# Packing a 64-wide remainder tile into two column halves of TensorE, with a new head and tail, in a two-GEMM SiLU kernel

## Chip, cores and metric

One core of a Trainium2 chip. The metric is the device time of one execution in microseconds (us). An execution with a profile also gives a span, from its first to its last instruction; here the time is about 1.8 us longer than the span (134.19 against 132.4 before).

## The reference

```python
B, S, D, F = 1, 2048, 640, 1728        # all bf16
def reference(x, w1, w2):
    h = jnp.einsum("bsd,df->bsf", x, w1)
    h = silu(h)
    return jnp.einsum("bsf,fd->bsd", h, w2)
```

F = 1728 is 13 tiles of 128 and one of 64. This remainder is what the change is about.

## The kernel before

A scheduler orders the instructions of each engine and sets the waits. The parts that matter (cuts marked):

```python
WARM_MMS = 10
...
zt = wpool.tile([P, 512], dt_in, name="zt")
nc.vector.memset(zt[:], 0.0)
for i in range(WARM_MMS):                      # keep TensorE busy until x has landed
    nc.tensor.matmul(ps_w[:, :], lhsT=zt[:, 0:P], rhs=zt[:, :], ...)
nc.vector.memset(w1_sb[:, :, F:F_PAD], 0.0)    # the 14th tile is padded from 64 to 128
nc.gpsimd.memset(w2_sb[F_REM:P, FT - 1, :], 0.0)
# head: x rows 0-511, then w1 in pieces of 384 columns, then the other x by transposing DMA
for dt in range(DT):                           # DT = 5
    ... four 128x128 transposes into psT (two buffers) ...
    if k % 2 == 0: nc.vector.tensor_copy(out=dst, in_=psT[:, :])
    else:          nc.scalar.activation(out=dst, in_=psT[:, :], func=ACT.Copy)
# first GEMM: 4 chunks of 512 rows x FT = 14 tiles x 5 matmuls
for (s0, w) in g1_chunks:
    for ft in range(FT):
        for dt in range(DT):
            nc.tensor.matmul(ps[:, :w], lhsT=w1_sb[:, dt, f0 : f0 + P],
                             rhs=xT_sb[:, dt, s0 : s0 + w], ...)
        nc.scalar.activation(out=sig[:, :w], in_=ps[:, :w], func=ACT.Sigmoid)
        nc.vector.tensor_tensor(out=gT_sb[:, ft, s0 : s0 + w], in0=ps[:, :w], in1=sig[:, :w], op=ALU.mult)
# second GEMM: 16 row blocks x 2 halves of 320 columns x 14 matmuls
for st in range(ST):
    for ci, (e0, en) in enumerate(e_chunks):
        for ft in range(FT):
            nc.tensor.matmul(ps2[:, :en], lhsT=gT_sb[:, ft, s0 : s0 + P],
                             rhs=w2_sb[:, ft, e0 : e0 + en], ...)
        ... evict on ScalarE (ci 0) or VectorE (ci 1) ...
    nc.sync.dma_start(out=of[s0 : s0 + P, :], in_=o_sb[:])
```

## Time and profile before

| | before |
|---|---|
| time, median | 134.19 us (6 runs when I predicted; 133.94 us over 16 runs later) |
| span of the profiled execution | 132.4 us |
| busy: PE, DVE, ACT | 127.7, 48.4, 43.2 us |
| PE idle before its two large groups | 0.0 us |

PE is TensorE, PEld its weight loads, DVE VectorE, ACT ScalarE, POOL GpSimd, SP SyncE; a "q" behind a name is the engine's sequencer, and "issue" is time in which the engine waited for nothing that the profile shows. A busy PE says little by itself, since matmuls overlap one another (one of 512 columns is recorded as 379 ns long, and the next starts 216 ns after it). The useful lines are the chain that ended last and the spacing of the matmuls in it. The prediction quotes and reads them.

TensorE begins at a slower pace. The ten warm-ups of 512 columns took 424 ns each, against 216 later, and transposes start 107 ns apart up to 6.21 us and 55 ns apart from 6.61 on. In between, at 6.36 us, the trace's raw record of the granted clock at full speed begins. This is the "rise of the clock" below; "cold" is before it. What sets its time is not shown.

### The profile page before, as it was taken

The page shows a single profiled execution, that of the slowest core. Times are in us where ns is not written, and L with a number is a line of the kernel's source. Part 1 is how long each engine was busy: PE and PEld are TensorE (multiplying, and loading weights), DVE is VectorE, ACT ScalarE, POOL GpSimd, SP SyncE. Part 2 cuts the span into 40 slices and gives each one's busy share as a digit, 9 for nine tenths or more (in the row PEclk, how much of TensorE's full clock was granted, in tenths as well). Part 3 has the DMA queues.
Part 4 walks back from the last instruction along what each step waited for, and adds up shares of the span by engine and source line. Part 5 has one row for each costly group of instructions (what it writes and reads, how often), then busy time and mean ns, then how long its engine had stood idle before and what let it go on. Part 6 is the DMA issues. An engine that isn't in the chain of part 4 may idle for free.

```text
span 132.4 us, 1881 instructions
## 1 busy us (share of the span) xinstructions
PE 127.7 (96%) x758; PEld 74.2 (56%) x758; DVE 48.4 (37%) x78; ACT 43.2 (33%) x76; POOL 1.3 (1%) x7
## 2 busy tenths in 40 slices
PE   6999999999999999999999999999999999999990
PEld 2454444444444444444457777777777777777760
DVE  1136666666666666666661001111110111111101
ACT  4055555555555555555551111100111111011110
POOL 4000000000000000000000000000000000000000
PEclk9999999999999999999999999999999999999999
DMA  3999446549900000000000111110011111101111
GB/s 89 353 330 228 104 104 60 117 92 290 357 9 2 0 5 2 0 0 0 0 0 5 50 50 50 50 51 18 35 50 50 50 54 50 49 2 48 54 50 50
DMA packets 16040, 9.78 MB, mean 74 GB/s; under 512 B 9184, under 2 KB 16032, under 8 KB 16032
## 3 DMA queue, kind: packets, MB, share of 16 engines
q1 hardware_dynamic: 16032, 9.67, 25.8%
q8 instruction: 6, 0.10, 0.3%
q14 instruction: 2, 0.02, 0.0%
HBM read 5.08 MB, written 2.62 MB: 58 GB/s over the span
## 4 chain that ended last, share of the span: by engine, by line
PE 96%; DVE 1%; issue 0%; DVEq 0%
PE ps L193 46%; PE ps L171 46%; PE ps L90 3%; PE psT L147 1%; DVE o_sb L203 0%; DVE xT_sb L154 0%; DVE zt L87 0%; DVE warm L77 0%; DVEq L203 0%
## 5 line engine op out<-in xcount | busy, mean ns | idle before, releaser
L193 PE MATMUL ps<-w_sb,gT_sb 128*128 128x320 bf16 x448 | 61.0, 299 | 0.0
L171 PE MATMUL ps<-xT_sb,w_sb 128*128 128x512 bf16 x280 | 60.9, 379 | 0.0
L193 PEld LDWEIGHTS <-gT_sb 128*128 128x128 bf16 x448 | 43.8, 98 | 17.2
L180 DVE TENSOR_TENSOR gT_sb<-ps,sig 128x512 bf16<-128x512 f32 x56 | 38.8, 692 | 22.5 <-ACT sig L179 22.5
L171 PEld LDWEIGHTS <-w_sb 128*128 128x128 bf16 x280 | 27.3, 98 | 32.8 <-issue 0.2
L179 ACT ACTIVATE sig<-ps 128x512 bf16<-128x512 f32 x56 | 33.5, 598 | 27.2 <-PE ps L171 27.2
L203 DVE CAST o_sb<-ps 128x320 bf16<-128x320 f32 x16 | 7.9, 492 | 52.2 <-PE ps L193 52.2
L201 ACT ACTIVATE o_sb<-ps 128x320 bf16<-128x320 f32 x16 | 7.0, 438 | 51.8 <-PE ps L193 51.8
L90 PE MATMUL ps<-zt 128*128 128x512 bf16 x10 | 4.4, 631 | 1.2 <-DVE zt L87 1.2
L154 DVE COPY xT_sb<-psT 128x512 bf16<-128x512 bf16 x3 | 1.3, 425 | 5.7 <-PE psT L147 5.7
L90 PEld LDWEIGHTS <-zt 128*128 128x128 bf16 x10 | 1.3, 143 | 3.4 <-issue 2.2
L156 ACT ACTIVATE xT_sb<-psT 128x512 bf16<-128x512 bf16 x2 | 1.2, 598 | 4.8 <-PE psT L147 4.8
L147 PEld LDWEIGHTS <-xn_sb 128*128 128x128 bf16 x20 | 1.8, 118 | 1.2 <-issue 0.8
L147 PE MATMUL psT<-ident,xn_sb 128*128 128x128 bf16 x20 | 2.1, 255 | 0.1
L78 ACT ACT_TABLE_LOAD x1 | 1.3, 1283 | 0.7 <-PEq L219 0.7
L101 POOL MEMSET w_sb<- 64x640 bf16 x1 | 0.6, 632 | 0.1
L77 DVE MEMSET warm<- 128x4 f32 x1 | 0.1, 62 | 0.8 <-PEq L219 0.8
masks.py:199 POOL TENSOR_SCALAR_AFFINE_SELECT ident<-ident 128x128 bf16<-128x128 bf16 x1 | 0.3, 294 | 0.1
L87 DVE MEMSET zt<- 128x256 uint32 x1 | 0.3, 272 | 0.0
L78 ACT ACTIVATE warm<-warm 128x4 f32<-128x4 f32 x1 | 0.2, 206 | 0.0
masks.py:197 POOL MEMSET ident<- 128x128 bf16 x1 | 0.2, 205 | 0.3 <-POOLq L219 0.3
L99 DVE MEMSET w_sb<- 128x160 uint32 x1 | 0.2, 192 | 0.0
(4 smaller groups left out, 0.4 us busy)
## 6 DMA issues: line engine op xcount, KB each, us to landing
out_dram<-o_sb SPq DMA_DIRECT2D x16, 160.0 KB, 1.8
w_sb<-in_w_dram SPq DMA_DIRECT2D x1, 2080.0 KB, 9.0
w_sb<-in_w_dram SPq DMA_DIRECT2D x4, 480.0 KB, 6.7
xn_sb<-in_x_dram SPq DMA_DIRECT2D x1, 640.0 KB, 4.3
w_sb<-in_w_dram SPq DMA_DIRECT2D x1, 240.0 KB, 7.0
xT_sb<-in_x_dram SPq DMA_TRANSPOSE x15, 2.8
w_sb<-in_w_dram SPq DMA_DIRECT2D x1, 80.0 KB, 8.6
```

Source lines behind the costliest of these rows:

```text
L78: nc.scalar.activation(out=warm[:], in_=warm[:], func=ACT.Sigmoid)
L90: nc.tensor.matmul(ps_w[:, :], lhsT=zt[:, 0:P], rhs=zt[:, :], start=(i == 0), stop=(i == WARM_MMS - 1),)
L101: nc.gpsimd.memset(w2_sb[F_REM:P, FT - 1, :], 0.0)
L147: nc.tensor.transpose(out=psT[:, i * P : (i + 1) * P], in_=xn_sb[:, sa // P + i, dt * P : (dt + 1) * P], identity=ident[:, :],)
L154: nc.vector.tensor_copy(out=dst, in_=psT[:, :])
L156: nc.scalar.activation(out=dst, in_=psT[:, :], func=ACT.Copy)
L171: nc.tensor.matmul(ps[:, :w], lhsT=w1_sb[:, dt, f0 : f0 + P], rhs=xT_sb[:, dt, s0 : s0 + w], start=(dt == 0), stop=(dt == DT - 1),)
L179: nc.scalar.activation(out=sig[:, :w], in_=ps[:, :w], func=ACT.Sigmoid)
L180: nc.vector.tensor_tensor(out=gT_sb[:, ft, s0 : s0 + w], in0=ps[:, :w], in1=sig[:, :w], op=ALU.mult,)
L193: nc.tensor.matmul(ps2[:, :en], lhsT=gT_sb[:, ft, s0 : s0 + P], rhs=w2_sb[:, ft, e0 : e0 + en], start=(ft == 0), stop=(ft == FT - 1),)
L201: nc.scalar.activation(out=o_sb[:, e0 : e0 + en], in_=ps2[:, :en], func=ACT.Copy)
L203: nc.vector.tensor_copy(out=o_sb[:, e0 : e0 + en], in_=ps2[:, :en])
```

## The change

It intends to (1) compute the 64-wide tile of two chunks at the same time, in the two column halves of the array; (2) shorten the head, with fewer warm-up matmuls, a smaller first piece of w1 and all copies of transposed x on VectorE; (3) shorten the tail by splitting the last row block into 512 and 128 columns with a store each. The second GEMM gets a second copy of w2's remainder, `w2b_sb`, zero in partitions 0 to 63, for the chunks whose remainder now lies in partitions 64 to 127. The core of the diff (many cuts, marked):

```diff
-WARM_MMS = 10
-W1_PIECE_COLS = 384
+WARM_MMS = 8
+W1_PIECES = [128, 256, 384, 384]
+LAST_ST_SPLIT = [512, 128]
...
-        nc.vector.memset(zt[:], 0.0)
+        nc.gpsimd.iota(zt32[:], pattern=[[1, max(P, WARM_N) // 2]], base=1, channel_multiplier=P)
...
+        if PST_COPY_ACT and k % 2 == 1:          # PST_COPY_ACT = 0
+            nc.scalar.activation(out=dst, in_=psT[:, :], func=ACT.Copy)
+        else:
+            nc.vector.tensor_copy(out=dst, in_=psT[:, :])
...
+    for (ca, cb) in pairs:                        # (1, 2) and (3, 0)
+        ps_p = psum1.tile([P, 512], mybir.dt.float32, name="ps1")
+        for dt in range(DT):
+            for h, s0 in ((0, sa), (HP, sb)):     # HP = 64
+                nc.tensor.matmul(
+                    ps_p[h : h + HP, :],
+                    lhsT=w1_sb[:, dt, fl * P : fl * P + HP],
+                    rhs=xT_sb[:, dt, s0 : s0 + 512], ...)
+        ... one sigmoid and one multiply for both halves, into gP ...
...
+                if ft < fl:
+                    lh = gT_sb[:, ft, s0 : s0 + P]
+                    rh = w2_sb[:, ft, e0 : e0 + en]
+                else:
+                    g, k = where[s0 // 512]
+                    lh = g[:, s0 % 512 : s0 % 512 + P]
+                    rh = (w2b_sb if k else w2_sb[:, fl, :])[:, e0 : e0 + en]
...
+            if st == last_st:
+                nc.sync.dma_start(out=of[s0 : s0 + P, e0 : e0 + en], in_=o_sb[:, e0 : e0 + en])
```

More of the change, by code (lines that the diff above doesn't have):

```diff
@@ L10 @@
 ALU = mybir.AluOpType
-WARM_MMS = 10
-C0_SUB = 512
-W1_PIECE_COLS = 384
-PE_TRANSPOSE_CHUNK0 = 1
+WARM_MMS = 8
+WARM_N = 512
+W1_PIECES = [128, 256, 384, 384]
+LAST_ST_SPLIT = [512, 128]
+COLPACK = 1
+PST_COPY_ACT = 0
 @with_exitstack
@@ L28 @@
     P = nc.NUM_PARTITIONS
+    HP = P // 2
     xf = x.flatten_outer_dims()
@@ L42 @@
     dt_in = x.dtype
+    dup = F_REM == HP
     chunks = []
@@ L52 @@
     c0_tiles = wc0 // P
-    c0_sub = min(wc0, max(P, (C0_SUB // P) * P)) if PE_TRANSPOSE_CHUNK0 else wc0
-    assert wc0 % c0_sub == 0
+    pairs = []
+    if COLPACK and dup and len(chunks) % 2 == 0 and all(w == 512 for _, w in chunks):
+        order = list(range(1, len(chunks))) + [0]
+        for i in range(0, len(order), 2):
+            pairs.append((order[i], order[i + 1]))
+    packed_chunks = set(c for pr in pairs for c in pr)
     e_chunks = []
@@ L62 @@
         e += n
+    if LAST_ST_SPLIT and sum(LAST_ST_SPLIT) == D and all(v % 32 == 0 and 0 < v <= 512 for v in LAST_ST_SPLIT):
+        e_chunks_last = []
+        e = 0
+        for v in LAST_ST_SPLIT:
+            e_chunks_last.append((e, v))
+            e += v
+    else:
+        e_chunks_last = e_chunks
     wpool = ctx.enter_context(tc.tile_pool(name="wpool", bufs=1))
@@ L74 @@
     gT_sb = gpool.tile([P, FT, S], dt_in, name="gT_sb")
+    ident = wpool.tile([P, P], dt_in, name="ident")
+    make_identity(nc, ident)
+    xn_sb = wpool.tile([P, c0_tiles, D], dt_in, name="xn_sb")
+    if WARM_MMS > 0:
+        zt32 = wpool.tile([P, max(P, WARM_N) // 2], mybir.dt.int32, name="zt32")
+        nc.gpsimd.iota(zt32[:], pattern=[[1, max(P, WARM_N) // 2]], base=1, channel_multiplier=P)
+        zt = zt32.bitcast(dt_in)
+        ps_w = psum2.tile([P, 512], mybir.dt.float32, name="ps2")
+        for i in range(WARM_MMS):
+            nc.tensor.matmul(
+                ps_w[:, :WARM_N],
+                lhsT=zt[:, 0:P],
+                rhs=zt[:, :WARM_N],
+                start=(i == 0),
+                stop=(i == WARM_MMS - 1),
+            )
     warm = wpool.tile([P, 4], mybir.dt.float32, name="warm")
@@ L78 @@
     nc.scalar.activation(out=warm[:], in_=warm[:], func=ACT.Sigmoid)
-    if PE_TRANSPOSE_CHUNK0:
-        ident = wpool.tile([P, P], dt_in, name="ident")
-        make_identity(nc, ident)
-        xn_sb = wpool.tile([P, c0_tiles, D], dt_in, name="xn_sb")
-    if WARM_MMS > 0:
-        zt = wpool.tile([P, 512], dt_in, name="zt")
-        nc.vector.memset(zt[:], 0.0)
-        ps_w = psum2.tile([P, 512], mybir.dt.float32, name="ps2")
-        for i in range(WARM_MMS):
-            nc.tensor.matmul(
-                ps_w[:, :],
-                lhsT=zt[:, 0:P],
-                rhs=zt[:, :],
-                start=(i == 0),
-                stop=(i == WARM_MMS - 1),
-            )
-    if F_PAD > F:
+    if F_PAD > F and not dup:
         nc.vector.memset(w1_sb[:, :, F:F_PAD], 0.0)
@@ L101 @@
         nc.gpsimd.memset(w2_sb[F_REM:P, FT - 1, :], 0.0)
+    w2b_sb = wpool.tile([P, D], dt_in, name="w2b_sb")
+    nc.gpsimd.memset(w2b_sb[0:HP, :], 0.0)
     x3 = xf.rearrange("s (dt p) -> s dt p", p=P)
-    if PE_TRANSPOSE_CHUNK0:
-        for sa in range(0, wc0, c0_sub):
-            sb = sa + c0_sub
-            nc.sync.dma_start(
-                out=xn_sb[:, sa // P : sb // P, :],
-                in_=xf[s0c0 + sa : s0c0 + sb, :].rearrange("(st p) d -> p st d", p=P),
-            )
-    else:
-        for dt in range(DT):
-            nc.sync.dma_start(
-                out=xT_sb[:, dt, s0c0 : s0c0 + wc0],
-                in_=x3[s0c0 : s0c0 + wc0, dt, :],
-                transpose=True,
-            )
-    w1r = w1.rearrange("(dt p) f -> p dt f", p=P)
-    f_piece = max(P, (W1_PIECE_COLS // P) * P)
-    for f0 in range(0, F, f_piece):
-        f1 = min(F, f0 + f_piece)
+    nc.sync.dma_start(
+        out=xn_sb[:, :, :],
+        in_=xf[s0c0 : s0c0 + wc0, :].rearrange("(st p) d -> p st d", p=P),
+    )
+    w1r = w1.rearrange("(dt p) f -> p dt f", p=P)
+    f_bounds = []
+    f0 = 0
+    for wdt in W1_PIECES:
+        if f0 >= F:
+            break
+        f1 = min(F, f0 + max(P, (wdt // P) * P))
+        f_bounds.append((f0, f1))
+        f0 = f1
+    if f0 < F:
+        f_bounds.append((f0, F))
+    for (f0, f1) in f_bounds:
         nc.sync.dma_start(out=w1_sb[:, :, f0:f1], in_=w1r[:, :, f0:f1])
@@ L138 @@
         nc.sync.dma_start(out=w2_sb[0:F_REM, FT - 1, :], in_=w2[F_FULL:F, :])
-    if PE_TRANSPOSE_CHUNK0:
-        psum_t = ctx.enter_context(tc.tile_pool(name="psum_t", bufs=2, space=bass.MemoryType.PSUM))
-        k = 0
-        for sa in range(0, wc0, c0_sub):
-            for dt in range(DT):
-                psT = psum_t.tile([P, c0_sub], dt_in, name="psT")
-                for i in range(c0_sub // P):
-                    nc.tensor.transpose(
-                        out=psT[:, i * P : (i + 1) * P],
-                        in_=xn_sb[:, sa // P + i, dt * P : (dt + 1) * P],
-                        identity=ident[:, :],
-                    )
-                dst = xT_sb[:, dt, s0c0 + sa : s0c0 + sa + c0_sub]
-                if k % 2 == 0:
-                    nc.vector.tensor_copy(out=dst, in_=psT[:, :])
-                else:
-                    nc.scalar.activation(out=dst, in_=psT[:, :], func=ACT.Copy)
-                k += 1
@@ L159 @@
-    g1_chunks = []
-    for ci, (s0, w) in enumerate(chunks):
-        if ci == 0 and PE_TRANSPOSE_CHUNK0:
-            for sa in range(0, w, c0_sub):
-                g1_chunks.append((s0 + sa, c0_sub))
-        else:
-            g1_chunks.append((s0, w))
-    for (s0, w) in g1_chunks:
-        for ft in range(FT):
-            f0 = ft * P
-            ps = psum1.tile([P, 512], mybir.dt.float32, name="ps1")
-            for dt in range(DT):
+        nc.sync.dma_start(out=w2b_sb[HP:P, :], in_=w2[F_FULL:F, :])
@@ new lines @@
+    psum_t = ctx.enter_context(tc.tile_pool(name="psum_t", bufs=2, space=bass.MemoryType.PSUM))
+    k = 0
+    for dt in range(DT):
+        psT = psum_t.tile([P, wc0], dt_in, name="psT")
+        for i in range(c0_tiles):
+            nc.tensor.transpose(
+                out=psT[:, i * P : (i + 1) * P],
+                in_=xn_sb[:, i, dt * P : (dt + 1) * P],
+                identity=ident[:, :],
+            )
+        dst = xT_sb[:, dt, s0c0 : s0c0 + wc0]
+        if PST_COPY_ACT and k % 2 == 1:
+            nc.scalar.activation(out=dst, in_=psT[:, :], func=ACT.Copy)
+        else:
+            nc.vector.tensor_copy(out=dst, in_=psT[:, :])
+        k += 1
@@ new lines, in gemm1_tile @@
+    def gemm1_tile(s0, w, ft):
+        f0 = ft * P
+        ps = psum1.tile([P, 512], mybir.dt.float32, name="ps1")
+        for dt in range(DT):
+            nc.tensor.matmul(
+                ps[:, :w],
+                lhsT=w1_sb[:, dt, f0 : f0 + P],
+                rhs=xT_sb[:, dt, s0 : s0 + w],
+                start=(dt == 0),
+                stop=(dt == DT - 1),
+            )
+        sig = work.tile([P, 512], dt_in, name="sig")
+        nc.scalar.activation(out=sig[:, :w], in_=ps[:, :w], func=ACT.Sigmoid)
+        nc.vector.tensor_tensor(
+            out=gT_sb[:, ft, s0 : s0 + w],
+            in0=ps[:, :w],
+            in1=sig[:, :w],
+            op=ALU.mult,
+        )
@@ new lines @@
+    for ci, (s0, w) in enumerate(chunks):
+        n_ft = FT - 1 if ci in packed_chunks else FT
+        for ft in range(n_ft):
+            gemm1_tile(s0, w, ft)
+    fl = FT - 1
+    assert pairs and e_chunks[0][1] == e_chunks[1][1] and len(e_chunks) == 2
+    gP = []
+    for (ca, cb) in pairs:
+        sa, wa = chunks[ca]
+        sb, wb = chunks[cb]
+        ps_p = psum1.tile([P, 512], mybir.dt.float32, name="ps1")
+        for dt in range(DT):
+            for h, s0 in ((0, sa), (HP, sb)):
@@ L171 @@
                 nc.tensor.matmul(
-                    ps[:, :w],
-                    lhsT=w1_sb[:, dt, f0 : f0 + P],
-                    rhs=xT_sb[:, dt, s0 : s0 + w],
+                    ps_p[h : h + HP, :],
+                    lhsT=w1_sb[:, dt, fl * P : fl * P + HP],
+                    rhs=xT_sb[:, dt, s0 : s0 + 512],
                     start=(dt == 0),
                     stop=(dt == DT - 1),
+                    skip_group_check=True,
                 )
-            sig = work.tile([P, 512], dt_in, name="sig")
@@ L179 @@
-            nc.scalar.activation(out=sig[:, :w], in_=ps[:, :w], func=ACT.Sigmoid)
-            nc.vector.tensor_tensor(
-                out=gT_sb[:, ft, s0 : s0 + w],
-                in0=ps[:, :w],
-                in1=sig[:, :w],
-                op=ALU.mult,
-            )
-    for st in range(ST):
+        sig = work.tile([P, 512], dt_in, name="sig")
+        nc.scalar.activation(out=sig[:, :], in_=ps_p[:, :], func=ACT.Sigmoid)
+        g = gpool.tile([P, 512], dt_in, name=f"gP{ca}")
+        nc.vector.tensor_tensor(out=g[:, :], in0=ps_p[:, :], in1=sig[:, :], op=ALU.mult)
@@ new lines @@
+        gP.append(g)
+    where = {}
+    for pi, (ca, cb) in enumerate(pairs):
+        where[ca] = (gP[pi], 0)
+        where[cb] = (gP[pi], 1)
+    st_per_chunk = [range(s0 // P, (s0 + w) // P) for (s0, w) in chunks]
+    st_order = []
+    late = []
+    if pairs:
+        la, lb = pairs[-1]
+        late = [la, lb]
+    for ci in range(len(chunks)):
+        if ci not in late:
+            st_order += list(st_per_chunk[ci])
+    for ci in late:
+        st_order += list(st_per_chunk[ci])
+    last_st = st_order[-1]
@@ L188 @@
+    for st in st_order:
         s0 = st * P
         o_sb = opool.tile([P, D], dt_in, name="o_sb")
-        for ci, (e0, en) in enumerate(e_chunks):
-            ps2 = psum2.tile([P, 512], mybir.dt.float32, name="ps2")
+        ec = e_chunks_last if st == last_st else e_chunks
+        ps2s = [psum2.tile([P, 512], mybir.dt.float32, name="ps2") for _ in ec]
+        for ci, (e0, en) in enumerate(ec):
             for ft in range(FT):
+                if ft < fl:
+                    lh = gT_sb[:, ft, s0 : s0 + P]
+                    rh = w2_sb[:, ft, e0 : e0 + en]
+                else:
+                    g, k = where[s0 // 512]
+                    lh = g[:, s0 % 512 : s0 % 512 + P]
+                    rh = (w2b_sb if k else w2_sb[:, fl, :])[:, e0 : e0 + en]
@@ L193 @@
                 nc.tensor.matmul(
-                    ps2[:, :en],
-                    lhsT=gT_sb[:, ft, s0 : s0 + P],
-                    rhs=w2_sb[:, ft, e0 : e0 + en],
+                    ps2s[ci][:, :en],
+                    lhsT=lh,
+                    rhs=rh,
                     start=(ft == 0),
@@ L199 @@
                 )
+        for ci, (e0, en) in enumerate(ec):
             if ci % 2 == 0:
-                nc.scalar.activation(out=o_sb[:, e0 : e0 + en], in_=ps2[:, :en], func=ACT.Copy)
+                nc.scalar.activation(out=o_sb[:, e0 : e0 + en], in_=ps2s[ci][:, :en], func=ACT.Copy)
             else:
-                nc.vector.tensor_copy(out=o_sb[:, e0 : e0 + en], in_=ps2[:, :en])
-        nc.sync.dma_start(out=of[s0 : s0 + P, :], in_=o_sb[:])
+                nc.vector.tensor_copy(out=o_sb[:, e0 : e0 + en], in_=ps2s[ci][:, :en])
+            if st == last_st:
+                nc.sync.dma_start(out=of[s0 : s0 + P, e0 : e0 + en], in_=o_sb[:, e0 : e0 + en])
+        if st != last_st:
+            nc.sync.dma_start(out=of[s0 : s0 + P, :], in_=o_sb[:])
 _INS = ['x', 'w1', 'w2']
```

## The prediction

> **What bounds the kernel now.** I began with the chain that ended last, because on one core it says directly which engine sets the end.
>
> ```profile
> PE 96%; DVE 1%; issue 0%; DVEq 0%
> PE ps L193 46%; PE ps L171 46%; PE ps L90 3%; PE psT L147 1%; DVE o_sb L203 0%; DVE xT_sb L154 0%; DVE zt L87 0%; DVE warm L77 0%; DVEq L203 0%
> ```
>
> TensorE (PE) is on 96% of the chain: half first GEMM (L171), half second (L193). So a cut counts only where it takes time from PE's stream or from the two ends, before PE starts and after it stops. The chain of waits in order of time shows those ends:
>
> ```profile
> 0.90 0.28 DVE zt L87
> ...
> 1.23 4.45 PE ps L90 x10
> 5.67 0.44 PE psT L147 x4
> ...
> 6.14 0.44 DVE xT_sb L154
> ...
> 6.61 0.38 PE psT L147 x4
> 7.00 0.22 PE ps L171
> 7.21 0.68 PE psT L147 x8
> 7.90 60.31 PE ps L171 x279
> 68.21 60.87 PE ps L193 x448
> ...
> 129.15 0.49 DVE o_sb L203
> ```
>
> Three stretches: a head of 7.90 us; 60.31 + 60.87 us of matmuls without a gap; and from 129.07 to the end of the span at 132.4 a tail of 3.3 us (last eviction, last store, closing barrier). Start to start, the 512-column matmul takes 60.31/279 = 216 ns and the 320-column one 60.87/448 = 136 ns. The durations in the groups below (379 and 299 ns) overlap each other and must not be summed as time on the path:
>
> ```profile
> L193 PE MATMUL ps<-w_sb,gT_sb 128*128 128x320 bf16 x448 | 61.0, 299 | 0.0
> L171 PE MATMUL ps<-xT_sb,w_sb 128*128 128x512 bf16 x280 | 60.9, 379 | 0.0
> L203 DVE CAST o_sb<-ps 128x320 bf16<-128x320 f32 x16 | 7.9, 492 | 52.2 <-PE ps L193 52.2
> L154 DVE COPY xT_sb<-psT 128x512 bf16<-128x512 bf16 x3 | 1.3, 425 | 5.7 <-PE psT L147 5.7
> L156 ACT ACTIVATE xT_sb<-psT 128x512 bf16<-128x512 bf16 x2 | 1.2, 598 | 4.8 <-PE psT L147 4.8
> ```
>
> Idle before the two big PE groups is 0.0, so no buffer or transfer holds PE back in the middle. VectorE (DVE) and ScalarE (ACT) are a third busy and wait for PE. In the head, the timeline of the first 22 us says what holds the transposes:
>
> ```profile
> 5.09 0.11 PEld L147 LDWEIGHTS <-xn_sb 128*128 128x128 bf16 x1 [0.32 <-DMA xn_sb<-in_x_dram]
> 5.47 1.53 PE L147 MATMUL psT<-ident,xn_sb 128*128 128x128 bf16 x12
> ```
>
> The x rows had landed by 5.09, but the first transpose starts at 5.47, when the tenth warm-up matmul lets go of the array. So two warm-up matmuls too many cost 5.47 - 5.09 = 0.38 us.
>
> [...]the ten warm-ups took (5.47 - 1.23)/10 = 424 ns each. [...]transposes from 5.47 start every 107 ns, those from 6.62 about every 55 ns, so the clock rose between 6.3 and 6.6, some 5.2 us after the first warm-up. [...]
>
> **The change part by part.**
>
> *Column packing of the last F tile.* F = 1728 is 13 tiles of 128 and one of 64. Now the 64-wide tile costs as much as a full one: 4 chunks x 5 matmuls = 20 x 216 = 4.32 us. After, these are 20 matmuls with 64 weight columns, in two groups of five pairs, one half of the pair writing PSUM partitions 0-63 and the other 64-127. If a pair overlaps fully, 10 x 216 = 2.16 us, saving 2.16. Against it: two changes of mode, since the two groups stand next to each other. A drain I estimate as a matmul's duration less its spacing, 379 - 216 = 163 ns, plus one exposed weight load of 98 ns (mean of L171's loads): 2 x 0.26 = 0.52 us. And imperfect overlap within a pair, by staggered starts and slower weight loads: I choose 40 ns for each of 10 pairs, 0.40 us. Net -2.16 + 0.52 + 0.40 = -1.24 us. Two ACT and two DVE instructions fewer in the epilogue are off the path and count zero. The first use of a packed tile in the second GEMM is its 14th matmul, 13 x 136 = 1.8 us after that GEMM begins; the epilogue of 598 + 692 ns fits, so no new wait.
>
> *Head.* Eight warm-ups instead of ten take 8 x 424 = 3.39 us. They now wait for an index fill on GpSimd (POOL) instead of the DVE fill that ended at 1.18. POOL writes its 64x640 bf16 memset in 632 ns, about 1 ns an element along a partition; for 256 int32 elements I estimate 0.3 to 0.6 us, starting near 1.0 once the identity's first memset is done. Warm-ups then run from about 1.5 to 4.9 us, and the first transposes start with the data at about 5.1: 0.37 us earlier. The copies of the transposes all go to DVE: 5 x (425 + 30) = 2.3 us from the end of the first group, not longer than before, when DVE and ACT alternated with 425 and 598 ns and the buffers (two) made the transposes wait. My schedule: transpose groups at 5.1, 5.5, 6.25, 6.7, 7.15; copies from 5.8, 6.2, 6.7, 7.1, 7.6; the matmuls that follow from about 7.4 instead of 7.7. Saving 0.36 at best; I count 0.25[...]. The first w1 piece is 128 columns in place of 384 and comes behind x in the same queue, so it lands earlier than now; w1 did not bind before and shouldn't now.
>
> *Middle.* The second GEMM keeps 448 matmuls of the same total columns. The zero half of w2 costs nothing more than before (it was zero padded already). The extra 80 KB load of w2's remainder is issued with the others near 30 us and wanted after 66 us: hidden.
>
> *Tail.* The last row block is split 512 + 128 rather than 320 + 320: 14 x (216 + 56) = 3.80 us against 28 x 136 = 3.80, with 56 ns taken from the warm transposes' spacing of about 55 ns at 128 columns. So PE is level. The last eviction shrinks by 192 columns x 1.04 = 0.20 us, to about 0.29. The last store carries 32 KB instead of 160 KB; the median landing of 1.8 us for 160 KB I take as mostly latency, so it gives at most 0.1. Count -0.20 us.
>
> *Sum:* -1.24 - 0.25 - 0.20 = -1.69 us, so 134.19 - 1.69 = 132.5 us. The 1.8 us by which the measured time exceeds the span I take as constant.
>
> **The rivals.** *The pairs don't overlap.* If the halves run one after the other, the 20 matmuls cost 4.32 us as before plus the drains: +0.5 instead of -1.24, giving about 134.2. For it: no trace here shows a pair, and both halves use all rows of the array. Against it: the halves write different partitions and have separate weights[...]. I give this 15%. Worse still, if each half counted as its own mode, 20 drains of 0.26 us would add 5 us: 139, 3%.
> *A new wait in the second GEMM.* Both PSUM tiles of a row block are now taken before either's matmuls. If the first matmul then waited for both old tiles to be emptied, PE would stall by about 0.5 us (the 492 ns eviction) at 15 boundaries, +8 us. Against it: a wait should belong to the first write into each tile, and each tile is emptied in about 0.5 us while the other one's 14 matmuls (14 x 136 = 1.9 us) run. 4%.
> *The clock stays low longer.* [...]+1.0, giving 133.5. The six runs of before differ by 0.4 us[...]. 20%.
> *All goes well.* Full overlap with cheap drains (-2.0), head -0.4, tail -0.3: 131.5, just at the 2% line of 134.19 x 0.98 = 131.5. 10%.
>
> **How the range and chances follow.** The centre is 132.5. Down, the best case is 131.5, hardly likely to the full, so I put the low end at 131.6; up, a failure of the packing with a working head gives 133.9, so 133.7 cuts off somewhat over a tenth. Faster by over 2% needs nearly every part at its best: 10%. Slower needs the mode change at each half or the new PSUM wait: about 5%. The rest, 85%, is within 2%.
>
> **What the changed profile would show.** Packing right: matmuls of shape 128*64 in pairs that start nearly together, ten steps of 216 to 260 ns, first GEMM plus packed part some 59 us in place of 60.3. Wrong: twenty steps of about 216 ns, or gaps of over 0.2 us between the halves. Head right: first transpose near 5.1, continuous matmuls from near 7.4, spacing 216 from the first. Wrong: warm-ups starting after 2 us[...]. Tail right: last eviction of 128 columns near 0.29 us and about 3.1 us from PE's end to the span's end. Middle: idle before the second GEMM's matmuls still 0.0; anything there makes the prediction wrong upward.

## The result, and the profile after

The changed kernel takes 131.04 us in the median of 8 runs (130.80 to 131.15), against 133.94 us for the kernel before (16 runs, 133.71 to 134.37). The ratio is 0.9775, with a 95% interval of 0.9762 to 0.9789. A ratio is the mean of one kernel's fast runs over the mean of the other's in the same rounds, so not quite the ratio of the medians. The gain of 2.9 us is larger than predicted, and 131.04 lies below the range (131.6 to 133.7). The 16 executions of the kernel before fall into two groups of eight, 133.71 to 133.85 and 134.02 to 134.37. The profiled one (134.19) is of the slower group, so differences to that profile come out somewhat larger than those of the medians.

The chain that ended last, shares of the span, after:

```profile
PE 93%; DMA 3%; DVE 1%; issue 0%; DVEq 0%
PE ps L256 47%; PE ps L180 43%; DMA xn_sb<-in_x_dram 3%; PE ps L210 2%; PE psT L164 1%; DVE xT_sb L173 0%; DVE o_sb L267 0%; DVEq L267 0%
```

PE still sets the end. The two stretches of 258 and 448 full matmuls are L180 (first GEMM) and L256 (second). The load of x, "DMA xn_sb", is on the chain now, where the warm-up was before, and the packed matmuls (L210) are 2%. The chain in order of time (start, length, what):

```profile
0.74 4.35 DMA xn_sb<-in_x_dram
...
5.14 0.61 PE psT L164 x4
...
6.63 0.22 PE ps L180
...
7.07 0.22 PE ps L180
...
7.53 55.71 PE ps L180 x258
63.24 2.28 PE ps L210 x20
65.52 60.97 PE ps L256 x448
...
126.58 0.29 DVE o_sb L267
```

Three things differ from before. The transposes begin at 5.14, with the data. Two matmuls of the first GEMM (6.63 and 7.07 in the chain) fit between transposes before the unbroken stream, where there was one. And 20 packed matmuls take 2.28 us, 114 ns each, where 20 of 216 ns took 4.31. The second GEMM takes the same 61 us. After its end the eviction of 128 columns takes 0.29 us instead of the 0.49 of 320 columns, and the last store lands sooner. The stores, KB each and median us from issue to landing, before (first line) and after:

```profile
out_dram<-o_sb SPq DMA_DIRECT2D x16, 160.0 KB, 1.8
out_dram<-o_sb SPq DMA_DIRECT2D x1, 32.0 KB, 1.4
```

The groups of packed matmuls and of their weight loads, and the last eviction, by form (busy us, mean ns, then idle before):

```profile
L210 PE MATMUL ps<-xT_sb,w_sb 128*64 128x512 bf16 x20 | 2.3, 381 | 0.0
L210 PEld LDWEIGHTS <-w_sb 128*64 128x64 bf16 x20 | 1.0, 110 | 1.2 <-issue 0.4
L267 DVE CAST o_sb<-ps 128x128 bf16<-128x128 f32 x1 | 0.3, 293 | 3.3 <-PE ps L256 3.3
```

One packed matmul lasts 381 ns, just as a full one (379); the trace models the ends of matmuls, so the spacing of the starts is the surer measure. The packed matmul isn't shorter; it has company. Very narrow windows of the PE timeline show it:

```profile
63.17 0.41 PE L210 MATMUL ps<-xT_sb,w_sb 128*64 128x512 bf16 x2
63.41 0.38 PE L210 MATMUL ps<-xT_sb,w_sb 128*64 128x512 bf16 x2
63.63 0.38 PE L210 MATMUL ps<-xT_sb,w_sb 128*64 128x512 bf16 x2
...
65.14 0.38 PE L210 MATMUL ps<-xT_sb,w_sb 128*64 128x512 bf16 x2
65.46 0.31 PE L256 MATMUL ps<-w_sb,gT_sb 128*128 128x320 bf16 x1
```

Each line is a pair ("x2"); the trace's own start times within a pair are 3.5 ns apart. Pairs follow every 216 ns. The last full matmul started at 62.865; one spacing later would be 63.081, and the first pair starts at 63.174: 0.093 us lost at the border, 0.024 more after the first pair, and 0.099 at the way out (65.141 + 0.216 to 65.456). The packed part costs 65.456 - 63.081 = 2.375 us instead of 4.31.

To account for the whole span, I take the "head" as the start of the second GEMM less its predecessors' matmuls at their own spacing: before 68.044 - 280 x 0.2157 = 7.65; after 63.081 - 260 x 0.2157 = 7.00. The "tail" runs from the start of the last matmul to the end of the span.

| term | predicted | measured in the traces |
|---|---|---|
| packing | -1.24 | 2.375 - 4.314 = -1.94 |
| head | -0.25 | 7.00 - 7.65 = -0.65 |
| tail, with the second GEMM | -0.20 | (3.02 - 3.62) + (60.81 - 60.72) = -0.51 |
| sum | -1.69 | -3.10 (span 132.38 to 129.28) |

### The profile page after: what moved, and what is told of

Read it like the earlier page. It is cut to its first block, busy times and chain, and to the rows that moved or that the text cites.

```text
span 129.3 us, 1875 instructions
## 1 busy us (share of the span) xinstructions
PE 124.6 (96%) x756; PEld 72.0 (56%) x756; DVE 47.1 (36%) x76; ACT 40.9 (32%) x72; POOL 2.3 (2%) x9
## 3 DMA queue, kind: packets, MB, share of 16 engines
HBM read 5.16 MB, written 2.62 MB: 60 GB/s over the span
## 4 chain that ended last, share of the span: by engine, by line
PE 93%; DMA 3%; DVE 1%; issue 0%; DVEq 0%
PE ps L256 47%; PE ps L180 43%; DMA xn_sb<-in_x_dram 3%; PE ps L210 2%; PE psT L164 1%; DVE xT_sb L173 0%; DVE o_sb L267 0%; DVEq L267 0%
## 5 line engine op out<-in xcount | busy, mean ns | idle before, releaser
L256 PE MATMUL ps<-w_sb,gT_sb 128*128 128x320 bf16 (+2 forms) x416 | 60.9, 299 | 0.0
L180 PE MATMUL ps<-xT_sb,w_sb 128*128 128x512 bf16 x260 | 56.6, 379 | 0.0
L256 PEld LDWEIGHTS <-gT_sb 128*128 128x128 bf16 x416 | 40.2, 98 | 16.8 <-issue 0.4
L189 DVE TENSOR_TENSOR gT_sb<-ps,sig 128x512 bf16<-128x512 f32 x52 | 36.0, 692 | 20.6 <-ACT sig L188 20.6
L180 PEld LDWEIGHTS <-w_sb 128*128 128x128 bf16 x260 | 25.4, 98 | 30.2
L267 DVE CAST o_sb<-ps 128x320 bf16<-128x320 f32 (+1 forms) x16 | 7.7, 480 | 52.3 <-PE ps L256 52.3
L265 ACT ACTIVATE o_sb<-ps 128x320 bf16<-128x320 f32 (+1 forms) x16 | 7.2, 448 | 53.1 <-PE ps L256 53.1
L256 PE MATMUL ps<-w_sb,gP 128*128 128x320 bf16 x16 | 4.8, 299 | 0.0
L256 PE MATMUL ps<-w2b_sb,gP 128*128 128x320 bf16 (+2 forms) x16 | 4.8, 299 | 0.0
L256 PEld LDWEIGHTS <-gP 128*128 128x128 bf16 x32 | 3.1, 98 | 1.3
L210 PE MATMUL ps<-xT_sb,w_sb 128*64 128x512 bf16 x20 | 2.3, 381 | 0.0
L210 PEld LDWEIGHTS <-w_sb 128*64 128x64 bf16 x20 | 1.0, 110 | 1.2 <-issue 0.4
```

The lines of the kernel that those rows point to most:

```text
L180: nc.tensor.matmul(ps[:, :w], lhsT=w1_sb[:, dt, f0 : f0 + P], rhs=xT_sb[:, dt, s0 : s0 + w], start=(dt == 0), stop=(dt == DT - 1),)
L210: nc.tensor.matmul(ps_p[h : h + HP, :], lhsT=w1_sb[:, dt, fl * P : fl * P + HP], rhs=xT_sb[:, dt, s0 : s0 + 512], start=(dt == 0), stop=(d ...
L256: nc.tensor.matmul(ps2s[ci][:, :en], lhsT=lh, rhs=rh, start=(ft == 0), stop=(ft == FT - 1),)
L265: nc.scalar.activation(out=o_sb[:, e0 : e0 + en], in_=ps2s[ci][:, :en], func=ACT.Copy)
L267: nc.vector.tensor_copy(out=o_sb[:, e0 : e0 + en], in_=ps2s[ci][:, :en])
```

## The experiments

Eleven kernels ran, all with a correct result. They ran on three chips, each beside the kernel before, so for small effects the ratio is surer than the median: by ratio e2, e4 and e9 are each about 0.5 us slower than the changed kernel, where the medians say 0.2, 0.3 and 0.6 (the intervals are about 0.3 us to either side). Edits are to the changed kernel. "Ratio" is to the kernel before in the same rounds; the changed kernel's is 0.9775.

| run | median us | ratio, 95% interval | span us |
|---|---|---|---|
| e1_nopack | 133.19 | 0.9943 (0.9926 to 0.9961) | 131.43 |
| e2_serial | 131.24 | 0.9810 (0.9789 to 0.9831) | 129.34 |
| e3_oldhead | 131.67 | 0.9832 (0.9815 to 0.9850) | 129.59 |
| e4_tail320 | 131.34 | 0.9811 (0.9794 to 0.9827) | 129.58 |
| e5_onetile | 133.46 | 0.9953 (0.9933 to 0.9972) | 131.62 |
| e6_switches | 133.09 | 0.9924 (0.9906 to 0.9943) | 131.34 |
| e7_w1old | 131.24 | 0.9793 (0.9771 to 0.9815) | 129.37 |
| e8_copyact | 131.30 | 0.9791 (0.9768 to 0.9814) | 129.58 |
| e9_warm10 | 131.66 | 0.9811 (0.9789 to 0.9834) | 129.87 |
| e10_rowpack | 129.39 | 0.9653 (0.9639 to 0.9667) | 127.56 |
| e11_xsplit | 131.58 | 0.9819 (0.9803 to 0.9836) | 129.38 |

### e1_nopack: the packing alone undone

```diff
-COLPACK = 1
+COLPACK = 0
-    dup = F_REM == HP
+    dup = False
```
(the pad of w1 is zeroed again, and the 14th tile runs as before)

> The changed kernel with the packing alone undone: the last, 64-wide F tile is computed as a full 128-column tile for each of the four chunks, as before. Head and tail stay changed. Theory: the trace of the changed kernel puts 20 packed matmuls in 2.38 us against 20 x 216 = 4.31 us, so the packing is worth 1.93 us; expected 131.04 + 1.9 = 133.0 us and a span near 131.2. Rival (the term of the recorded prediction, 1.24 us): 132.3 us.

Measured: 133.19 us, 2.15 more than the changed kernel, and a span of 131.43, also 2.15 more. Of that, 1.94 is the packing as read in the trace. The rest is a head 0.22 us longer, which the packing doesn't explain: in this execution the second piece of w1 landed late, at 7.99 us (7.12 in the changed kernel), and the matmul that needs it started at 8.04, 0.19 us after its place in the stream. The weight loads of the first GEMM show the wait:

```profile
L180 PEld LDWEIGHTS <-w_sb 128*128 128x128 bf16 x280 | 27.3, 98 | 32.9 <-DMA w_sb<-in_w_dram 0.5
```

The packing is the largest part of the gain, and the term of 1.24 was too small.

### e2_serial: the halves in series in the program

```diff
-        for dt in range(DT):
-            for h, s0 in ((0, sa), (HP, sb)):
+        for h, s0 in ((0, sa), (HP, sb)):
+            for dt in range(DT):
```

> The packed matmuls in another order, all five of the first half and then all five of the second, nothing else changed. Theory: the gain comes from two neighbours in the stream running at the same time in different halves of the array. Then only the pairs at the three borders (5th with 6th, 10th with 11th, 15th with 16th) overlap, 17 slots of 216 ns remain instead of 10, +1.5 us: 132.5 us. Rival: a matmul of 64 weight columns costs half of a full one by itself, 114 ns, wherever it stands; then 131.0 us as in the changed kernel.

My theory fell: 131.24 us, not 132.5. The instruction stream does hold five matmuls of columns 0-63, then five of 64-127. The narrow windows of the PE timeline show the first starts:

```profile
62.99 0.40 PE L210 MATMUL ps<-xT_sb,w_sb 128*64 128x512 bf16 x1
63.23 0.41 PE L210 MATMUL ps<-xT_sb,w_sb 128*64 128x512 bf16 x2
63.24 0.62 PE L210 MATMUL ps<-xT_sb,w_sb 128*64 128x512 bf16 x3
```

The second and third start 5 ns apart, at 63.235 and 63.240. Within one half, starts are 216 ns apart, so they are in different halves: the one at 63.240 is the sixth in the program, and it started before the program's third, at 63.450. From there two series run side by side, each every 216 ns; no exchange within one half shows. Semaphores confirm the exchange once more: the matmul that waits for the second group's PSUM tile, the program's eleventh, starts at 64.098, before the one that signals the end of the first group, the tenth, at 64.128. The packed part takes 2.62 us instead of 2.375, about one spacing more, for the first matmul that ran alone. This result by itself also fits the rival, a narrow matmul that simply costs half, so I took the partner away.

### e5_onetile: no partner

```diff
-    ps_p[h : h + HP, :]          # halves 0-63 and 64-127
+    ps_p[0:HP, :]                # all four chunks in columns 0-63, a PSUM bank each
```
(cut: each chunk now has its own sigmoid and multiply, and GpSimd zeroes the other half of each result)

> After the run with the halves one after the other came out as fast as the changed kernel (my theory had said 132.5), this run takes the partner away altogether: the 20 matmuls of 64 weight columns all use array columns 0-63 and write PSUM partitions 0-63, one bank for each chunk. Rival: a matmul of 64 weight columns costs half by itself; then 20 still take 2.3 us and the time stays at 131.1 us. Theory: the two halves of the array run as two streams, each at 216 ns a matmul, whatever the order in the program; then one stream alone takes 20 x 216 = 4.3 us, +2.1 us: 133.1 us.

Measured: 133.46 us. The chain in order of time:

```profile
63.42 4.43 PE ps L210 x20
```

Twenty matmuls of 64 columns without a partner take 4.43 us, 0.22 us each (4.53 with both borders, counted as the 2.375 was). A narrow matmul costs as much as a full one; the gain is the two halves running at once. The rival is out.

### e6_switches: twenty changes of shape

```diff
+            nc.tensor.matmul(ps_f[:, :], lhsT=w1_sb[:, dt, fi * P : fi * P + P], ...)
```
(inside the packed loop, after each pair; these ten full matmuls are taken out of the last two F tiles of chunk 3)

> The changed kernel with the packed pairs dealt out between full-width matmuls: each of the 10 pairs is followed by one of the ten full matmuls of the last two F tiles of chunk 3, so 20 changes between the 64-column and the 128-column shape instead of 2, with the same matmuls. Recorded prediction's term: 0.26 us a change, 18 x 0.26 = +4.7 us: 135.8 us. Theory from the trace of the changed kernel (93 ns into the packed part, 99 ns out of it, beyond the spacing of 216 ns): 18 x 0.1 = +1.8 us: 132.9 us. Third possibility: the gap at the border was something else and dealing out costs nothing: 131.1 us.

Measured: 133.09 us, and a span 131.339 - 129.284 = 2.06 us longer, for 18 more changes: 0.114 us each. The chain in order of time:

```profile
61.09 0.34 PE ps L215 x2
61.43 0.32 PE ps L223
61.75 0.34 PE ps L215 x2
```

A pair plus a full matmul takes 0.659 us (start of one pair to the next, 61.024 to 61.683) instead of 2 x 0.216: two changes cost 0.227. So a change of shape costs 0.11 us here, less than half of the 0.26 that the prediction allowed. 0.11 is about the length of one weight load (98 to 110 ns); what fills the time, these runs don't tell.

### e3_oldhead, e7_w1old, e8_copyact, e9_warm10: the head

e3 puts all of the old head back; the other three put back one part each.

```diff
-WARM_MMS = 8                              # e3, e9
+WARM_MMS = 10
-        nc.gpsimd.iota(...)               # e3
+        nc.vector.memset(zt[:], 0.0)
-PST_COPY_ACT = 0                          # e3, e8
+PST_COPY_ACT = 1
-W1_PIECES = [128, 256, 384, 384]          # e3, e7
+W1_PIECES = [384, 384, 384, 384]
```

> The changed kernel with the head of before: ten warm-up matmuls on zeros written by VectorE, w1 in pieces of 384 columns, transposed blocks copied by VectorE and ScalarE in turn. Theory: the head is worth 0.58 us by the traces (the unbroken matmul stream begins 0.36 us earlier and one matmul more stands in a gap before it): 131.6 us, unbroken stream of 512-column matmuls from about 7.7 us. Rival: the earlier rise of the clock in the changed kernel's trace is chance, and the head is worth the 0.25 us of the recorded prediction or less: 131.3 us or less.

> The changed kernel with w1 loaded in the pieces of before (384 columns each) and nothing else undone. Recorded prediction: w1 doesn't bind, so no change, 131.05 us. Theory from the run with the old head (first matmul on w1 at 6.62 us, just after its first piece landed at 6.57, the transposes behind it held up): the first matmul can't start before 6.6 us instead of 6.3 to 6.5, and the transposes queued behind it move with it, +0.1 to +0.3 us: 131.2 to 131.3 us.

> The changed kernel with the second and fourth transposed block copied by ScalarE (598 ns) instead of VectorE (423 ns). Recorded prediction: about even between the two. Theory: the fourth copy ends about 0.15 us later and holds one of the first matmuls by that much, the second is hidden because ScalarE can start while VectorE still copies the first: +0.0 to +0.2 us, 131.05 to 131.25 us.

> The changed kernel with ten warm-up matmuls instead of eight, nothing else. Recorded prediction's step: two too many hold the first transpose back by 0.38 us, here 10 x 0.424 + 1.38 = 5.6 us instead of 5.1, +0.4 us: 131.45 us, always. Theory after eight runs: only where the clock rises late. In the run with the old head it rose during the warm-up, and ten were done by 5.1; in most others it rose at 5.6 to 6.5. So 0 to +0.45 us by the execution, +0.2 to +0.4 in the median, 131.3 us, with a wider spread of single executions.

e3 took 131.67 us, 0.63 more than the changed kernel, as the theory said. Its profiled execution, though, is the fastest of the four and only 0.31 us longer than the changed kernel's, and it doesn't show the theory's head. In it the clock happened to rise early: the ten warm-ups ended by 5.1 us and the transposes within a group came 55 ns apart. So the warm-up held nothing back, and the next limits show. Timeline of that head:

```profile
6.61 0.10 PEld L179 LDWEIGHTS <-w_sb 128*128 128x128 bf16 x1 [0.38 <-DMA w_sb<-in_w_dram]
6.62 0.39 PE L179 MATMUL ps<-xT_sb,w_sb 128*128 128x512 bf16 x1 [0.20 <-DMA w_sb<-in_w_dram]
...
6.84 0.61 PE L163 MATMUL psT<-ident,xn_sb 128*128 128x128 bf16 x8
```

The first matmul on w1 waits for w1's first piece, and the last two groups of transposes stand behind it in PE's queue. So w1 does bind in the old head as soon as the clock is early, which the prediction denied. With the small piece the same matmul started at 6.29 in e2, where the clock was early too. The two early-clock heads, by the definition above, are 7.30 (e3) and 6.82 (e2): the new head is worth 0.48 us there, and 0.65 between the two profiled executions of before and after. A head without any edit varies by nearly as much with the clock: that of the changed kernel measured 6.82 in e2, where transposes came 55 ns apart from the first group on, and 7.18 in e5, where they were still 107 ns apart at 6.4 us.

e7 (131.24) and e8 (131.30) alone are at the edge of what timing tells; their traces show what was expected. In e7 the first matmul on w1 starts at 6.57 instead of 6.47 though its transposes came 0.05 to 0.08 earlier; in e8 a matmul waits from 7.75 to 7.92 for the longer copy on ScalarE (598 ns, 423 on VectorE).

e9 gave 131.66 in the median with single executions from 131.06 to 131.85, the wide spread that the theory expected. Its profile caught a late clock; the chain in order of time:

```profile
1.37 4.45 PE ps L104 x10
5.82 0.44 PE psT L164 x4
```

Ten cold warm-ups hold the first transpose until 5.61 us (start in the trace; the chain's line begins later because it ends the warm-up with its modelled length). The fastest execution, 131.06, is at the changed kernel's median. That fits two warm-ups too many costing nothing when the clock rises early, but no profile of that execution exists. By medians the single parts sum to 0.20 + 0.26 + 0.62 = 1.1 us, against 0.63 for all together; by ratios to 0.24 + 0.21 + 0.48 = 0.9, against 0.76. With these intervals the runs can't tell whether the parts add up.

### e4_tail320: the last row block 320 + 320

```diff
-LAST_ST_SPLIT = [512, 128]
+LAST_ST_SPLIT = [320, 320]
```

> The changed kernel with the last row block split 320 + 320 instead of 512 + 128, still two stores. Theory: of the tail's 0.53 us, 0.20 is the shorter last eviction (492 to 293 ns) and the rest a shorter landing of the last store (1.4 against 1.8 us) because it carries a fifth of the bytes; at 80 KB half of the landing's gain stays, so +0.35 us: 131.4 us. Rival: the landing became shorter only because the store was cut in two; then just the eviction comes back, +0.2 us: 131.2 us. Time on TensorE is the same in both (3.80 us).

Measured: 131.34 us, +0.30 (by ratio +0.48); the timing can't separate 0.35 from 0.2. The traces can. From issue to landing the last store took 1.77 us before (160 KB), 1.58 here (80 KB) and 1.45 in the changed kernel (32 KB). So of this run's loss 0.20 is the eviction (0.49 instead of 0.29) and 0.13 the landing. Both this run and the changed kernel cut the last block into two stores, so it is the bytes of the last one that count, about 0.32 us for 128 KB (410 GB/s), and the theory holds.

### e11_xsplit: is the landing of x the bound of the head?

```diff
-    nc.sync.dma_start(out=xn_sb[:, :, :], in_=...512 rows...)
+    for i in range(c0_tiles):
+        nc.sync.dma_start(out=xn_sb[:, i, :], in_=xf[s0c0 + i * P : s0c0 + (i + 1) * P, :])
```
(and five transposes and one copy of 640 columns for each piece)

> The changed kernel with the first 512 rows of x loaded in four pieces of 128 rows and transposed piece by piece (five transposes and one copy of 640 columns each, all on VectorE). It asks whether the landing of x at 5.1 us bounds the head. Theory: the first pieces land before the warm-up ends (about 4.8 us), so the transposes start 0.35 us earlier and the chain of four copies of about 0.53 us ends earlier too, -0.2 to -0.4 us: 130.75 us. Rival: four copies and the two buffers bound the chain just as before and every first matmul needs all four pieces, so nothing is gained or up to 0.3 us lost, since no first-GEMM matmul fits between the transposes any more.

The theory fell: 131.58 us, 0.54 more. The transposes began at 4.45 instead of 5.14, yet the chain in order of time shows where that went:

```profile
5.96 0.90 DVE xT_sb L169 x2
6.86 0.04 issue
6.90 56.28 PE ps L175 x260
```

The copies on DVE (0.90 us for the last two) now end the head, and all 260 matmuls come after them; none fits between the transposes. The head is 6.93 us, with an early clock, against 6.82 for e2: nothing gained, as the rival said. The span (129.38) explains only 0.1 of the 0.54, and that lies in the tail (1.10 us from the last landing to the end, 0.94 in the changed kernel). Why this kernel's time is 2.1 us above its span, not 1.8, I have not settled, so most of its loss stays open.

### e10_rowpack: the same done to the second GEMM

The runs so far say that halves of the array run at once for the price of 0.11 us a change. The second GEMM still pads its 64-row remainder with zeros, 32 full matmuls of 136 ns. Here the two row halves of `gP`, which belong to two chunks, are used as two row halves of the array, writing two different PSUM banks; all eight banks serve in turn, and four pairs make a phase.

```diff
+def rows(sl, tl, first, last):        # one pair: row halves 0-63 and 64-127
+    for h in (0, 1):
+        k0 = h * HP
+        w2t = w2b_sb[HP:P, :] if h else w2_sb[0:HP, fl, :]
+        nc.tensor.matmul(tl[h][:, :en], lhsT=gP[pi][k0 : k0 + HP, j * P : j * P + P],
+                         rhs=w2t[:, e0 : e0 + en], start=first, stop=last, ...)
...
+        full(s[0], t[0], True, False); full(s[1], t[1], True, False)   # 13 tiles each, two row blocks
+        for i in range(4):
+            rows(s[i], t[i], i >= 2, i < 2)    # ends slots 0, 1; begins slots 2, 3
+        full(s[2], t[2], False, True); full(s[3], t[3], False, True)
```

> A version that may beat both: the changed kernel with the same thing done to the second GEMM. The last 64 rows of its contraction, now a full matmul padded with zeros for each of 32 column groups, run as two row halves at once for two row blocks, in different PSUM banks, four such pairs in a phase, so 4 phases and 8 changes of shape. Theory from the runs so far: 32 x 136 = 4.34 us become 16 x 136 = 2.17, less 8 changes x 0.112 = 0.90: -1.27 us, 129.8 us. Rival (row halves, unlike column halves, run one after the other): +0.9 us, 131.9 us. Second rival: the eight PSUM banks, now all in turn, hold the matmuls up somewhere; then idle time before the second GEMM's matmuls, and no gain.

Measured: 129.39 us, ratio 0.9653, the fastest of all and faster than expected. Chain in order of time, then narrow windows of the PE timeline:

```profile
65.11 7.17 PE ps L249 x52
72.28 0.65 PE ps L265 x8
72.93 14.23 PE ps L249 x104
```

```profile
72.21 0.31 PE L265 MATMUL ps<-w_sb,gP 64*128 64x320 bf16 x1
72.22 0.31 PE L265 MATMUL ps<-w2b_sb,gP 64*128 64x320 bf16 x1
```

Eight row-half matmuls take 0.65 us; the two of a pair start within 4 ns, and pairs follow every 136 ns or so. From its first to its last matmul the second GEMM takes 59.49 us instead of 60.81, -1.32 against -1.27 expected. The rest comes from the head: the transposes now have eight PSUM banks instead of two and run without a break, and the head is 6.59 us, in an execution with an early clock (6.82 for e2). Now it is w1 that ends the head: its second piece landed at 7.14, and the fourth matmul waited for it until 7.19, 0.23 us after its place in the stream. Both rivals are out: row halves overlap, and there is no idle time before the matmuls of L249 and L265.

## Why the prediction was wrong

Its mechanism held, w1 apart: PE bounds, the pairs overlap, the middle has no new wait, and the listed signs appeared (128*64 shapes, first transpose near 5.1, stream from near 7.4, eviction of 0.29; from PE's end to the span's end 2.8 us, not 3.1). Of its rivals "All goes well" came, which it gave 10%, with more from head and tail than even that allowed. Sizes failed, all in the same direction.

- **Packing, "-2.16 + 0.52 + 0.40".** Right in its gross term. "Two changes of mode ... 2 x 0.26 = 0.52" was 0.22 with the slow first pair (e6: 0.11 a change over 18 more of them). "40 ns for each of 10 pairs" was nothing: pairs follow every 216 ns, starts 3.5 ns apart. The slower weight load was real per column (110 ns for 64 columns against 98 for 128) but lay under the running matmuls: pairs kept their 216 ns. Together 0.70 us, the largest error. Of the allowance, the part called a drain (379 - 216 = 163 ns) rested on the modelled end of a matmul and the 40 ns on no trace at all, and both were used as if measured. That the array drains at a change of shape is not shown; what a change costs is.
- **Head, "0.36 at best; I count 0.25".** The schedule was right: the third matmul starts at 7.37 where the prediction had 7.4. But it compared this with 7.73 before without counting that by then two matmuls are done instead of one, worth another 0.216. The remaining 0.06 is a wait behind them that shrank: before, a matmul stood from 8.17 to 8.26 for a copy by ScalarE (so the stream was not quite "without a gap"), after, 0.03. And w1 "did not bind before and shouldn't now" fits the two profiles but not every execution: its first piece held e3, its second e1 and e10. The profiled head gained 0.65; 0.48 at like, early clocks. The deduction from 0.36 to 0.25 was not needed for these two profiles, in which the clock rose at 6.36 us before and 5.59 after, but one for a late clock was not baseless: the same head measured 6.82 in e2 and 7.18 in e5. The rival of a clock that stays low, +1.0 us, equals about five 512-column matmuls at the cold spacing (424 - 216 = 0.21 us more each); that as many could run cold was a guess, and what the warm-up does to the time of the rise is not shown.
- **"Two warm-up matmuls too many cost 0.38".** True for the profiled execution, and for e9's; but it depends on when the clock rises, which varies between executions: in e3 the ten warm-ups had ended by 5.1 us, in e9 the first transpose waited until 5.61.
- **Tail, "at most 0.1. Count -0.20".** The eviction term was exact (0.20): 492 ns for 320 columns and 293 for 128 give its 1.04 ns a column. The landing gave 0.32 (1.77 to 1.45), not at most 0.1 and counted as none. "Mostly latency" is true of the whole (about 1.4 of 1.77 us by the line through the three sizes), but what the bytes add was not as small as it took. The level claim for PE held, within 0.09.
- **The starting level.** 134.19 was the median of six runs; sixteen gave 133.94. That alone is 0.25 us of the miss in absolute time. Four of the six were of the slower group, by chance as far as the record shows.
- **The upper end of the range.** It rests on a figure that its own terms don't give: "a failure of the packing with a working head" is 134.19 + 0.5 - 0.25 - 0.20 = 134.2, as its first rival says, not 133.9. This had no part in the miss, which lies at the other end.

## What to carry to other kernels

A remainder tile of half width cost a full matmul when it ran alone (4.53 us for 20, with both borders) and about half when a partner worked in the other half of the array (2.375); row halves overlapped in pairs as column halves did (0.65 us for eight), though a lone row half was not run. A change of shape cost 0.11 us, so gather the pairs into few phases. On a chain where one engine runs without gaps, count how many of its instructions are already done when the stream begins, not just when it begins. At the very end, the bytes of the last store (0.32 us for 128 KB) and the width of the last eviction (0.20 us for 192 columns) are on the path in full.
